# Attention and a two-layer network in one kernel: the third score tile turned by VectorE through DRAM, the fourth by direct moves from two queues, the first as one plain float32 product

## The chip, the core and the metric

The kernel runs on one core of a Trainium2 chip. The metric is the device time of one execution in microseconds (us); lower is better. The engines are TensorE (PE in the profile; PEld is its weight loads), VectorE (DVE), ScalarE (ACT), GpSimd (POOL) and SyncE (SP), which here only issues DMA transfers. They run side by side, each working through its own list of instructions in a fixed order, and wait for one another on semaphores.

## The reference

Attention with a decay that is computed from `f`, for 8 x 8 heads, 576 positions and 64 values per head, then a network of two layers with a leaky activation (cut):

```python
def _attn_ref(q, k, v, f):          # q, k, v: (8, 8, 576, 64); f: (8, 8, 576)
    scores = scale * np.matmul(q, k.transpose(0, 1, 3, 2))
    cum = np.cumsum(np.log(np.clip(f, 0.0001, 1.0)), axis=-1)
    decay = cum[:, :, :, None] - cum[:, :, None, :]
    scores = np.where(causal, -1000000000.0, scores + decay)
    attn = np.exp(scores - np.max(scores, axis=-1, keepdims=True))
    attn = attn / (np.sum(attn, axis=-1, keepdims=True) + 1e-09)
    return np.matmul(attn, v)
def _moe_ref(x, w_in, w_out, alpha):   # x: (4608, 512), w_in: (512, 2048), w_out: (2048, 512)
    h = x @ w_in
    g = np.maximum(h, 0.0) + alpha * np.minimum(h, 0.0)
    return g @ w_out
```

## The kernel before, in words

**Stages.** Attention goes in 32 stages, one for each pair of heads of a batch (`attention(n)`, `n` = 0 to 31). A stage has the rows of its scores in tiles: tiles 0 to 3 are 128 queries of one head against the 128, 256, 384 or 512 keys that the mask lets through, and the tail is the last 64 queries of both heads together against all 576 keys. For each tile TensorE forms the scores, VectorE adds the decay and mask (`Z`) and finds the row's extreme (L674, the tail L571), ScalarE takes the exponential and the row sums (L536).

**Terms.** From stage `NN` = 4 on, the float32 q and k are split into a high and a low part (ScalarE copies the high one, L496; GpSimd subtracts for the low one, L497), and a score is the sum of three products `Qh Kh`, `Qh Kl`, `Ql Kh`. Stages 0 to 3 use one plain float32 product.

**Turning.** The product with `v` needs the exponentials with keys on the partitions, so each 128 x 128 block has to be transposed. In a stage that is not turned all blocks are transposed by TensorE (L549, L718) into a PSUM bank and copied out by ScalarE (L545) or VectorE. In a *turned* stage (`NX[0] <= n < NX[1]`, stages 9 to 31) the fourth tile of both heads and the tail are written to a DRAM tile `ex` in one transfer (L694), read back in four with blocks of keys rearranged over the partitions (L696), and then turned by VectorE in blocks of 32 x 32 (L703, L706) into `eT3`. The order of keys differs from the plain one, so these stages load a `v` with rows in that order (`vt`). Tiles 0, 1, 2 and the tail's last 64 keys are still transposed by TensorE.

**Values.** The products with `v` of a stage are appended to the scores of tile 2 of the stage after it (`behind`, in `stretch`), and ScalarE copies them out (L755). They are scaled by the reciprocal row sums on VectorE (L767) and split into high and low part (L769 on ScalarE, L771 on GpSimd) into one of seven `xx` slots.

**The network.** `ffn1(b)` multiplies the four `xx` slots of a batch by the split `w_in`: 16 blocks of twelve products with 512 columns. Its batches are the filler: the planner gives them low priority, so that TensorE takes them when attention has nothing ready. A ninth pass takes the last 64 rows of all batches. Each block's result goes to DRAM (`hd`, L853). After attention its memory is given up (`change`), `w_out` is loaded and converted in eight chunks (`load_w_out`, L987 to L1014, mostly VectorE and ScalarE), and `ffn2` does the second layer in 18 units of four groups.

**The order of the work.** `Plan` holds every operation with its engine, estimated nanoseconds, key, dependencies and buffers. `Plan.run` simulates the engines: it takes the operation that can start first, at equal start that of lowest key, and issues it. Thus the order on each engine is fixed when the program is built. Transfers also occupy a common channel in this plan, at 220 and later 280 GB/s; the plan counts only transfers of SP in it. `Ring` and `Store` are pools of buffers; a buffer is taken when an operation starts and is free when its last user ends. Once the last stage that is not turned is through, `swap` hands buffers that turned stages no longer need to other rings.

Of the kernel before, what the change touches and what calls it, by code (L numbers as in the profile page):

```python
# [23 lines left out]
QW = 640  # L24
# [6 lines left out]
NX = (9, B * NP)  # L31
NZ = 1+9
NQ = 4
HURRY = 25
# [52 lines left out]
class Plan:  # L87
# [30 lines left out]
    def run(self):  # L118
# [7 lines left out]
        while left:  # L126
# [63 lines left out]
def attention_moe(  # L190
    ctx: ExitStack,
    tc: tile.TileContext,
    qk: bass.AP,
    vv: bass.AP,
    vt: bass.AP,
    f: bass.AP,
# [19 lines left out]
    ex = [dram.tile([3, 128, 512], F32, name=f"ex{i}") for i in range(2)]  # L216
# [34 lines left out]
    rvr = ring(sp, 2, [128, 8, 2, D], F32, "vr")  # L251
# [12 lines left out]
    re = ring(sp, 3, [128, S], F32, "e")  # L264
# [170 lines left out]
    def load_n(n, held):  # L435
# [8 lines left out]
        l_qk = [op("SP", 450, lambda c0=c0, c1=c1: sy.dma_start(bqk.t[:, c0:c1], qk[b, p][:, c0:c1]), kq, dq, [bqk], kb=(c1 - c0) / 2)  # L444
                for c0, c1 in (((0, QW), (QW, QW + S)) if n < NQ else ((0, QW + S),))]
# [43 lines left out]
        if n < NN:  # L489
            held += [bqk]  # L490
            return l_qk, rz, rt, bZ, [(q_, k_)]
# [3 lines left out]
        for hi, lo, raw, w, ld in ((Qh, Ql, q_, QW, l_qk[0]), (Kh, Kl, k_, S, l_qk[-1])):  # L495
            o1 = op("ACT", c_acs(w), lambda hi=hi, raw=raw: ac.activation(hi(), raw(), AF.Copy), kc, [ld], [bqk, bQ])  # L496
# [3 lines left out]
        return out, rz, rt, bZ, [(Qh, Kh), (Qh, Kl), (Ql, Kh)]  # L500
# [3 lines left out]
    def attention(n):  # L504
# [8 lines left out]
        rdy, rz, rt, bZ, terms = load_n(n, held)  # L513
        bv, turned = Buf(rvr), NX[0] <= n < NX[1]
        if turned:
            l_v = op("SP", 400, lambda: sy.dma_start(bv.t, vt[b, p]), kl + 12, [o_scan], [bv], kb=512)
        else:
            l_v = op("SP", 400, lambda: sy.dma_start(bv.t[:, 0:5], vv[b, p]), kl + 1, [o_scan], [bv], kb=320)
# [3 lines left out]
        t2_of = (lambda h: bT2[h].t[:, h]) if turned else (lambda h: bT2[h].t[:, 0:3, 0:128])  # L522
        b3, bT3 = Buf(re3), Buf(rT3)
        if turned:
            bm = Buf(rm3)
# [26 lines left out]
        e2, e3 = [[], []], []  # L552
# [3 lines left out]
        def tail(st):  # L556

            bt = b3 if turned else Buf(re)
# [18 lines left out]
            if turned:  # L577
                return bt, nt
# [8 lines left out]
        e4 = None  # L587
# [49 lines left out]
        def stretch(tiles, st):  # L637

            part = [(i, bool(i >= 2 and len(tiles) > 1), 128 if i == 1 else 0) for i in tiles]
            bS = [[Buf(rS) for _ in range(2)] for _ in range(1 + part[-1][1])]  # L640

            def prods():
                for i, g, c0 in part:
                    w = 128 * i + 128
                    for c, (q, k) in enumerate(terms):
                        for h in range(2):
                            r = slice(64 * h, 64 * h + 64)
                            mm(bS[g][h].t[:, c0 : c0 + w], q()[r, 128 * i : 128 * i + 128], k()[r, 0:w], c == 0, c == len(terms) - 1)
# [4 lines left out]
            s = op("PE", ns, lambda: (prods(), vp()), st, rdy + vd, [x for y in bS for x in y] + held + vb)  # L653
            s_0.append(s)
            if after:
                value_ops.append(s)
            done(s)
            if n == NE - 1 and tiles[-1] == 3:
                op("-", 0, lambda: setattr(rS, "least", 4), 0, [s])
            return {i: (bS[g], c0) for i, g, c0 in part}, s  # L660

        def tile(h, i, st, bS, s, c0):
# [3 lines left out]
            b1 = b3 if i == 3 else Buf(res if i < 2 else re)  # L666
            at = (lambda t: t[:, 512 * h : 512 * h + 512]) if i == 3 else (lambda t: t)
# [21 lines left out]
            if i == 3 and turned:  # L689
                if h == 0:  # L690
                    return
                key = k0 + 7.8
                d = ex[n % 2]
                o_ = op("SP", 400, lambda: sy.dma_start(d.rearrange("g q k -> q g k"), b3.t[:, 0:1536].rearrange("p (g k) -> p g k", g=3)),  # L694
                        key, [be[0][3][1], nm, nt], [b3], kb=768)
                got = [op("SP", 400, lambda k=k: sy.dma_start(  # L696
                    bm.t[32 * k : 32 * k + 32], d[:, :, 128 * k : 128 * k + 128].rearrange("g (a c) s -> c (g a) s", c=32)),
                    key + 0.1, [o_], [bm], kb=256) for k in range(4)]
                for g in range(3):
# [9 lines left out]
                    e3.append(op("DVE", c_tr(512) + 100 * (g == 2), turn, k0 + 13.5, got, [bm, bT3]))  # L709
# [18 lines left out]
        def prods_of(r, out):  # L728

            def pv():  # L730
                both = []
                o = out()
                for h in range(2):
# [3 lines left out]
                    else:  # L737
                        t3 = bT3.t[:, :, 192 * h : 192 * h + 192]
                        head = [(j, 0, 128, e2_[:, j]) for j in range(3)]
                        if turned:  # L740
                            both.append(head + [(j + 4, 128, 320, t3[:, j]) for j in range(3)] + [(3, 256, 320, bT4.t[:, 64 * h : 64 * h + 64])]
                                        + [(7, 128, 320, t3[:, 3])])
# [15 lines left out]
        v_deps = lambda: e1 + e2[0] + e2[1] + e3 + [e4, o_zero, l_v]  # L758
# [40 lines left out]
        if n < NE - 1 or n == B * NP - 1:  # L799
            vb, vp, vd, done = values()  # L800
            done(op("PE", ns_v + 250, vp, k0 + 9.6 - hurry, vd, vb))
        else:
            behind.append(values)
# [77 lines left out]
    o_ct = [op("POOL", c_po(S) + 60, lambda h=h: sides(h), kc_ + 3, [o_cq]) for h in range(2)]  # L881
    for n in range(NX[0], B * NP):
        attention(n)
        if n == NX[0]:
            def swap():
                for st, t in [(rT2b.store, t2s[:, i, 0:768].rearrange("p (h j q) -> p h j q", h=2, q=128)) for i in range(2)] + [
                        (re3.store, t2s[:, 2:4].rearrange("p a n -> p (a n)"))]:
                    st.free.append((plan.t, len(st.items)))
                    st.items.append(t)

            op("-", 0, swap, 0, [value_ops[-1]])
# [78 lines left out]
    def load_w_out(c):  # L970
        key = 1e5 + c
# [175 lines left out]
_ARGS = ["qk", "vv", "vt", "f", "w_in", "w_out", "alpha"]  # L1147
# [37 lines left out]
```

## Time and profile before

| | |
|---|---|
| median of 3 runs | 1058.59 us (1058.38 to 1058.63) |
| the profiled execution's own time | 1056.91 us |
| its span | 1054.7 us |
| granted TensorE clock | 0.995 |
| transfers of `ex` | 23 writes of 768 KB, 92 reads of 192 KB |
| transfers of q and k | 8 in the first four stages, 28 of 608 KB after them |
| HBM read, written | 125.41 MB, 66.61 MB |

A group row of the profile has the line, engine, operation, `out<-in` by the program's names, the shapes and a count; then the busy time and the mean ns of one; then the engine's idle time just ahead and what ended it. A timeline row has the start and the length in us. In the chain that ended last each row is the start and length of a piece of work that the next one had to follow. `eT__114` in the rows is the second buffer of `e3`, which `swap` added.

### The profile page before, as it was taken

Reading aid. Unit: us, or ns where it says so; the run is one execution under the profiler, and the core shown is the slowest. Engines: PE = TensorE matmul, PEld = TensorE weight load, DVE = VectorE, ACT = ScalarE, POOL = GpSimd, SP = SyncE. Lnnn points to the kernel's source line nnn. Section 1 sums busy time; section 2 is a strip of 40 time slices with the busy share of each in tenths; the row PEclk is TensorE's granted clock in tenths of the full one; section 3 lists DMA queues with packets and bytes.
Section 4 is the critical chain, followed back from the end, with each engine's and each line's share of the span. In section 5 each row is a group of like instructions: output and inputs, shape, how many; then the busy total and the mean of one; then the engine's idle time right before and its main releaser. Section 6 shows DMA issues by size and latency. Waiting matters only on the chain.

```text
span 1054.7 us, 21382 instructions
## 1 busy us (share of the span) xinstructions
PE 1041.1 (99%) x7680; PEld 901.6 (85%) x7680; DVE 797.8 (76%) x1772; ACT 661.7 (63%) x1546; POOL 283.6 (27%) x411
## 2 busy tenths in 40 slices
PE   8889999999999999999999999999999999999998
PEld 4578888778778787877788888899999999999998
DVE  6887876667667666757753697789889888989994
ACT  6878885677676767676754566656464554645551
POOL 6586765355344444453510000000000000000000
PEclk9989999999999999999999999999999999999999
DMA  5867757877687678787764667364434434344411
GB/s 182 255 207 219 237 185 215 251 222 222 211 254 237 201 222 249 243 209 217 216 171 149 211 223 237 141 210 134 136 121 143 137 121 142 121 139 126 135 61 41
DMA packets 148820, 193.87 MB, mean 184 GB/s; under 512 B 16723, under 2 KB 98122, under 8 KB 148714
## 3 DMA queue, kind: packets, MB, share of 16 engines
q1 hardware_dynamic: 148425, 192.31, 60.4%
q8 instruction: 60, 0.98, 0.4%
q14 instruction: 47, 0.38, 0.1%
q10 hardware_dynamic: 288, 0.20, 0.1%
HBM read 125.41 MB, written 66.61 MB: 182 GB/s over the span
## 4 chain that ended last, share of the span: by engine, by line
PE 96%; DVE 2%; POOL 1%; ACT 0%; issue 0%; DVEq 0%
PE bank L342 90%; PE bank L549 5%; PE bank L402 1%; PE bank L718 0%; DVE wr L332 0%; DVE wr L329 0%; DVE xs L767 0%; PE bank L618 0%; DVE wr L333 0%; DVE e L674 0%; POOL Z L469 0%; ACT es L536 0%; DVE eT L544 0%; DVE eT__114 L544 0%; POOL wi L338 0%
## 5 line engine op out<-in xcount | busy, mean ns | idle before, releaser
L342 PE MATMUL bank<-xx,wi 128*128 128x512 f32 x1728 | 427.0, 397 | 0.0
L342 PEld LDWEIGHTS bank<-xx,wi 128*128 128x128 f32 x1728 | 314.7, 188 | 65.8 <-issue 4.9
L851 DVE SCALAR_TENSOR_TENSOR hs<-bank,sa,hs 128x512 f32<-128x512 f32 x96 | 71.7, 747 | 117.2 <-ACT hs L849 116.7
L342 PE MATMUL bank<-wot,xx 128*128 128x256 f32 x1008 | 123.9, 283 | 0.0
L342 PE MATMUL bank<-wi,xx 128*128 128x256 f32 x1008 | 123.9, 283 | 0.0
L342 PEld LDWEIGHTS bank<-wot,xx 128*128 128x128 f32 x1008 | 122.3, 192 | 0.0
L342 PEld LDWEIGHTS bank<-wi,xx 128*128 128x128 f32 x1008 | 122.3, 192 | 0.0
L849 ACT ACTIVATE hs<-bank,ab 128x512 f32<-128x512 f32 x96 | 65.9, 686 | 70.1 <-PE bank L342 69.5
L469 POOL TENSOR_TENSOR Z<-Z,tri 128x384 f32<-128x384 f32 x64 | 61.4, 966 | 106.6 <-DVE Z L453 90.3
L536 ACT ACTIVATE e<-e,st 128x384 f32<-128x384 f32 (+2 forms) x127 | 84.8, 672 | 2.9 <-issue 1.1
L771 POOL TENSOR_TENSOR xx<-xs,xx 128x256 fp32r<-128x256 f32 x64 | 49.2, 779 | 131.6 <-ACT xx L769 131.6
L1073 ACT ACTIVATE xx<-gx 128x1024 fp32r<-128x1024 f32 x48 | 50.8, 1058 | 30.6 <-PE bank L342 12.7
L342 PE MATMUL bank<-eT,vr 128*64 128x192 f32 (+3 forms) x896 | 69.3, 303 | 0.0
L1076 DVE TENSOR_TENSOR xx<-gx,xx 128x1024 fp32r<-128x1024 f32 x48 | 58.5, 1219 | 8.2 <-ACT xx L1073 8.2
L342 PE MATMUL bank<-wi,gh 128*128 128x256 f32 x504 | 62.4, 283 | 0.0
L342 PE MATMUL bank<-wot,gh 128*128 128x256 f32 x504 | 62.4, 283 | 0.0
L342 PEld LDWEIGHTS bank<-eT,vr 128*64 128x64 f32 x896 | 55.1, 137 | 8.1
L342 PEld LDWEIGHTS bank<-wot,gh 128*128 128x128 f32 x504 | 61.4, 192 | 0.1
L342 PEld LDWEIGHTS bank<-wi,gh 128*128 128x128 f32 x504 | 61.3, 192 | 0.0
L755 ACT ACTIVATE xs<-bank 128x320 f32<-128x320 f32 (+1 forms) x64 | 25.5, 409 | 56.9 <-PE bank L342 29.3
L497 POOL TENSOR_TENSOR Ql<-rqk,Qh 128x640 fp32r<-128x640 f32 x28 | 45.4, 1620 | 57.4 <-ACT Qh L496 44.5
L342 PE MATMUL bank<-Kh,Qh 64*128 64x128 f32 (+1 forms) x280 | 60.4, 365 | 0.0
(156 smaller groups left out, 1889.1 us busy)
## 6 DMA issues: line engine op xcount, KB each, us to landing
hd<-hs SPq DMA_DIRECT2D x144, 256.0 KB, 3.6
wx<-hd SPq DMA_DIRECT2D x47, 512.0 KB, 3.7
wr<-ex SPq DMA_DIRECT2D x92, 192.0 KB, 4.8
rqk<-in_qk_dram SPq DMA_DIRECT2D x28, 608.0 KB, 4.4
hr<-hd SPq DMA_DIRECT2D x25, 512.0 KB, 4.0
vr<-in_vt_dram SPq DMA_DIRECT2D x23, 512.0 KB, 5.3
ex<-e SPq DMA_DIRECT2D x12, 768.0 KB, 5.2
ex<-eT__114 SPq DMA_DIRECT2D x11, 768.0 KB, 4.5
```

The source lines that it names most:

```text
L342: pe.matmul(o, lhsT, rhs, start=start, stop=stop)
L402: op("PE", 800, lambda: [pe.matmul(bw.t, wbf[:, 0:128], wbf, start=True, stop=True) for _ in range(3)], -200, [o_wbf], [bw])
L469: m1 = op("POOL", c_po(128 * 3), lambda z4=z4: po.tensor_tensor(z4()[:, 6:9], z4()[:, 0:3], tb(3), ALU.add), kc + 0.1, got + [o_mask], [bZ])
L497: o2 = op("POOL", c_po(w), lambda hi=hi, lo=lo, raw=raw: po.tensor_tensor(lo(), raw(), hi().bitcast(F32), ALU.subtract), kc, [o1], [bqk, bQ])
L536: ex = op("ACT", c_exp(w), lambda: ac.activation(at(bt.t)[:, :w], at(bt.t)[:, :w], AF.Exp, bias=lo()[:, col : col + 1], scale=-1.0, accum_ ...
L549: pe.transpose(t[:, c : c + 128], src[:, 128 * j : 128 * j + 128], ident)
L755: xs_ops[r].append(op("ACT", c_act(w_), lambda: ac.activation(bxs[r].t, bP.t[:, 0:w_], AF.Copy), st, [pvo], [bP, bxs[r]]))
L771: xl = op("POOL", c_po(256), lambda r=r, t0=t0: po.tensor_tensor(bx.t[:, 1, t0 : t0 + 256], bxs[r].t[:, 0:256], bx.t[:, 0, t0 : t0 + 256]. ...
L849: cp = op("ACT", c_act(512), lambda bh=bh, bs=bs, fc=fc: ac.activation(bs.t, bh.t, AF.Relu, scale=ab[:, fc : fc + 1]), -1000, [last, o_sg] ...
L851: cp = op("DVE", c_dve(512), lambda bh=bh, bs=bs, fc=fc: ve.scalar_tensor_tensor(bs.t, bh.t, sa[:, fc : fc + 1], bs.t, ALU.mult, ALU.add), ...
L1073: his.append(op("ACT", c_acs(128 * GW * (j1 - j0)), lambda j0=j0, j1=j1, src=src, o_=o_: ac.activation(o_(0, j0, j1), src(), AF.Copy), key ...
L1076: rdy.append(op("DVE", c_dve(128 * GW * (j1 - j0)), lambda j0=j0, j1=j1, src=src, o_=o_: ve.tensor_tensor(o_(1, j0, j1), src(), o_(0, j0, ...
```

## The change

- The turned stages begin with stage 10 (`NX`), as does the way in which `Z` is filled there (`NZ`).
- In turned stages tile 2 of both heads is written to DRAM (`ex2`), read back in four transfers and turned by VectorE in one instruction of 768 columns; TensorE's transposes and ScalarE's copies of it are gone. The tail's last 64 keys are transposed alone.
- The fourth tile and the tail no longer pass through DRAM: 16 transfers, each of 32 partitions, move them straight to the place where the reads put them; they are issued in turn by SP and GpSimd.
- In turned stages tile 0's scores are one plain float32 product of the raw q and k, which are held until then.
- In turned stages tiles 2 and 3 come first, and 0 and 1 after them with the values of the stage before.
- From stage 4 on q and k come in two transfers (`qk1`, `qk2`); in turned stages `v` comes in two (`vt`, `vu`), in a single buffer that has ten blocks, three of them for the key order of tile 2.
- `swap` comes ahead of the first turned stage and waits for the values of the stage before; it now hands out the memory of `e` and `v` too.
- In `Plan` transfers of every queue count in the channel. Chunks 4 to 7 of `w_out` get keys among the groups of the first `ffn2` unit (`WC`).

The diff, cut to its core:

```diff
-NX = (9, B * NP)
-NZ = 1+9
+NX = (10, B * NP)
+NZ = 1+10
+WC = 4
...
-            if o.eng == "SP":
+            if o.kb:
...
-    ex = [dram.tile([3, 128, 512], F32, name=f"ex{i}") for i in range(2)]
+    ex2 = [dram.tile([2, 128, 384], F32, name=f"exs{i}") for i in range(2)]
...
+        else:
+            l_qk = [op("SP", 500, lambda: sy.dma_start(bqk.t[:, 0:1024].rearrange("p (c n) -> p c n", c=2), qk1[b, p].rearrange("c p n -> p c n")), kq, dq, [bqk], kb=400),
+                    op("SP", 500, lambda: sy.dma_start(bqk.t[:, 1024:], qk2[b, p]), kq, dq, [bqk], kb=96)]
...
         if turned:
-            l_v = op("SP", 400, lambda: sy.dma_start(bv.t, vt[b, p]), kl + 12, [o_scan], [bv], kb=512)
+            l_v = [op("SP", 500, lambda: sy.dma_start(bv.t[:, 0:8].rearrange("p (c j) h d -> p c (j h d)", c=2), vt[b, p].rearrange("c p n -> p c n")), kl + 12, [o_scan], [bv], kb=400),
+                   op("SP", 500, lambda: sy.dma_start(bv.t[:, 8:10], vu[b, p]), kl + 12, [o_scan], [bv], kb=128)]
...
+                tt = op("PE", 109, lambda: pe.transpose(bTt.t[0:64, 0:128], tail_of(bt.t)[:, 512:S], ident), st + 1.3, [nt, o_id], [bTt, bt])
+                e4 = op("ACT", c_act(128), lambda: ac.activation(bT4.t[0:64], bTt.t[0:64, 0:128], AF.Copy), st + 1.31, [tt], [bTt, bT4])
...
-                    for c, (q, k) in enumerate(terms):
+                    these = [raw[:2]] if raw and i == 0 else terms
+                    for c, (q, k) in enumerate(these):
...
-            after = behind.pop() if tiles == (2,) and behind else None
+            after = behind.pop() if tiles == ((0, 1) if turned else (2,)) and behind else None
...
-                key = k0 + 7.8
-                d = ex[n % 2]
-                o_ = op("SP", 400, lambda: sy.dma_start(d.rearrange("g q k -> q g k"), b3.t[:, 0:1536].rearrange("p (g k) -> p g k", g=3)),
-                        key, [be[0][3][1], nm, nt], [b3], kb=768)
-                got = [op("SP", 400, lambda k=k: sy.dma_start(
-                    bm.t[32 * k : 32 * k + 32], d[:, :, 128 * k : 128 * k + 128].rearrange("g (a c) s -> c (g a) s", c=32)),
-                    key + 0.1, [o_], [bm], kb=256) for k in range(4)]
+                key = k0 + 4.8
+                src = lambda a, k: b3.t[32 * a : 32 * a + 32, 0:1536].rearrange("p (g s) -> p g s", g=3)[:, :, 128 * k : 128 * k + 128]
+                dst = lambda a, k: bm.t[32 * k : 32 * k + 32].rearrange("p (g a) s -> p g a s", a=4)[:, :, a]
+                got = []
+                for j in range(16):
+                    a, k = j // 4, j % 4
+                    q_, e_ = ((sy, "SP"), (po, "POOL"))[j % 2]
+                    got.append(op(e_, 600, lambda a=a, k=k, q_=q_: q_.dma_start(dst(a, k), src(a, k)), key + j / 100, [be[0][3][1], nm, nt], [b3, bm], kb=60))
...
+            if i == 2 and turned:
+                if h == 0:
+                    return
+                d2 = ex2[n % 2]
+                key = k0 + 2.2
+                o_ = op("SP", 500, lambda: sy.dma_start(d2.rearrange("h q k -> q h k"), be2.t.rearrange("p (h k) -> p h k", h=2)),
+                        key, [be[0][2][1], nm], [be2], kb=336)
+                got = [op("SP", 500, lambda k=k: sy.dma_start(
+                    bm2.t[32 * k : 32 * k + 32], d2[:, :, 96 * k : 96 * k + 96].rearrange("h (a c) s -> c (h a) s", c=32)),
+                    key + 0.1, [o_], [bm2], kb=148) for k in range(4)]
+                e2[0].append(op("DVE", c_tr(768), lambda: ve.transpose(
+                    bT2[0].t.rearrange("p s (a c) -> p a s c", c=32), bm2.t.rearrange("p a (s r) -> p a s r", r=32)), k0 + 8.4, got, [bm2, bT2[0]]))
                 return
...
-        k_ = (0, 2, 6, 8) if n < NE else (0, 2, 8, 6)
+        k_ = (0, 2, 6, 8) if n < NE else (7, 7.5, 0, 2) if turned else (0, 2, 8, 6)
-        for tiles in ((0, 1), (2,), (3,)) if n < NE else ((0, 1, 3), (2,)):
+        for tiles in ((0, 1), (2,), (3,)) if n < NE else ((2, 3), (0, 1)) if turned else ((0, 1, 3), (2,)):
...
-        key = 1e5 + c
+        key = 1e5 + c if c < WC else 2e6 + c // 2 - 0.5
```

More of the change, by code (lines that the diff above doesn't have):

```diff
@@ L193, in attention_moe @@
     qk: bass.AP,
+    qk1: bass.AP,
+    qk2: bass.AP,
     vv: bass.AP,
     vt: bass.AP,
+    vu: bass.AP,
     f: bass.AP,
@@ L250, in attention_moe @@
     rZ = Ring(Store([(sp.tile([128, 2, ZW], F32, name=f"Z{i}"), sp.tile([128, S], F32, name=f"Zt{i}")) for i in range(2)]))
-    rvr = ring(sp, 2, [128, 8, 2, D], F32, "vr")
+    vrt = sp.tile([128, 10, 2, D], F32, name="vr")
+    rvr = Ring(Store([vrt[:, 5 * i : 5 * i + 5] for i in range(2)]))
+    rvt = Ring(Store([]))
     rT1 = ring(sp, 3, [128, 384], F32, "eT1_")
@@ L263, in attention_moe @@
     rT4 = ring(sp, 2, [128, 128], F32, "eT4_")
-    re = ring(sp, 3, [128, S], F32, "e")
+    es_ = sp.tile([128, 3 * S], F32, name="e")
+    re = Ring(Store([es_[:, S * i : S * i + S] for i in range(3)]))
+    re2, rm2 = Ring(Store([])), Ring(Store([]))
     re3 = ring(sp, 1, [128, 1024 + S], F32, "e3_")
@@ L499, in load_n @@
         held.append(bQ)
-        return out, rz, rt, bZ, [(Qh, Kh), (Qh, Kl), (Ql, Kh)]
+        return out + l_qk, rz, rt, bZ, [(Qh, Kh), (Qh, Kl), (Ql, Kh)], (q_, k_, bqk) if n >= NX[0] else None
     waiting, behind, later_x, quick_ops, value_ops = [], [], [], [], []
@@ L521, in attention @@
         bT2 = [Buf(rT2b)] * 2 if turned else [Buf(rT2) for _ in range(2)]
-        t2_of = (lambda h: bT2[h].t[:, h]) if turned else (lambda h: bT2[h].t[:, 0:3, 0:128])
+        t2_of = (lambda h: bT2[h].t[:, :, 128 * h : 128 * h + 128]) if turned else (lambda h: bT2[h].t[:, 0:3, 0:128])
         b3, bT3 = Buf(re3), Buf(rT3)
         if turned:
-            bm = Buf(rm3)
+            bm, be2, bm2 = Buf(rm3), Buf(re2), Buf(rm2)
         bT4, bst = Buf(rT4), Buf(rst)
@@ L584, in tail @@
             return bt, nt
-        e4 = None
         xs_ops = [[], []]
@@ L637, in stretch @@
         def stretch(tiles, st):
-            part = [(i, bool(i >= 2 and len(tiles) > 1), 128 if i == 1 else 0) for i in tiles]
+            part = [(i, int(i >= 2 and i != tiles[0]), 128 if i == 1 else 0) for i in tiles]
             bS = [[Buf(rS) for _ in range(2)] for _ in range(1 + part[-1][1])]
@@ L665, in tile @@
             w = 128 * i + 128
-            b1 = b3 if i == 3 else Buf(res if i < 2 else re)
-            at = (lambda t: t[:, 512 * h : 512 * h + 512]) if i == 3 else (lambda t: t)
+            b1 = b3 if i == 3 else be2 if i == 2 and turned else Buf(res if i < 2 else re)
+            at = (lambda t: t[:, w * h : w * h + w]) if i == 3 or i == 2 and turned else (lambda t: t)
             col = 5 * h + i
@@ L738, in pv @@
                         t3 = bT3.t[:, :, 192 * h : 192 * h + 192]
-                        head = [(j, 0, 128, e2_[:, j]) for j in range(3)]
+                        head = [(j + 7 * turned, 0, 128, e2_[:, j]) for j in range(3)]
                         if turned:
-                            both.append(head + [(j + 4, 128, 320, t3[:, j]) for j in range(3)] + [(3, 256, 320, bT4.t[:, 64 * h : 64 * h + 64])]
-                                        + [(7, 128, 320, t3[:, 3])])
+                            both.append(head + [(j + 3, 128, 320, t3[:, j]) for j in range(3)] + [(2, 256, 320, bT4.t[:, 64 * h : 64 * h + 64])]
+                                        + [(6, 128, 320, t3[:, 3])])
                         else:
@@ L881, in attention_moe, with swap @@
     o_ct = [op("POOL", c_po(S) + 60, lambda h=h: sides(h), kc_ + 3, [o_cq]) for h in range(2)]
+    def swap():
+        for st, t in [(rT2b.store, t2s[:, i, 0:768].rearrange("p (s q) -> p s q", q=256)) for i in range(2)] + [
+                (re3.store, t2s[:, 2:4].rearrange("p a n -> p (a n)")), (re2.store, es_[:, 0:768]), (rvt.store, vrt),
+                (rm2.store, es_[:, 768:1536].rearrange("p (k s) -> p k s", s=96))]:
+            st.free.append((plan.t, len(st.items)))
+            st.items.append(t)
+    op("-", 0, swap, 0, [value_ops[-1]])
     for n in range(NX[0], B * NP):
         attention(n)
[L884 to L891, printed above, removed]
     done_a = [o for o in plan.ops if o not in set(x_late)]
@@ L1144, in attention_moe @@
     plan.run()
-_ARGS = ["qk", "vv", "vt", "f", "w_in", "w_out", "alpha"]
+_ARGS = ["qk", "qk1", "qk2", "vv", "vt", "vu", "f", "w_in", "w_out", "alpha"]
 def kernel(**inputs):
```

46 lines of the change are left out of this document (29 added, 17 removed).

## The prediction

> **What bounds the kernel now.** I read the page first: busy time by engine, then the chain that ended last.
>
> ```profile
> span 1054.7 us, 21382 instructions
> ...
> PE 1041.1 (99%) x7680; PEld 901.6 (85%) x7680; DVE 797.8 (76%) x1772; ACT 661.7 (63%) x1546; POOL 283.6 (27%) x411
> ...
> PE 96%; DVE 2%; POOL 1%; ACT 0%; issue 0%; DVEq 0%
> ```
>
> TensorE is busy for 99% of the span and carries 96% of the chain. A share can hide stages, so the windows view comes next; its columns are the length, busy time of TensorE, its weight loads, VectorE, ScalarE, GpSimd, then granted clock, DMA share and GB/s.
>
> ```profile
> 75.00:165.00 90.00, 90.00 (x761) 73.36 (x759) 66.52 (x160) 79.52 (x214) 60.03 (x73) 1.00 0.71 219
> 300.00:475.00 175.00, 175.00 (x1254) 139.27 (x1252) 115.89 (x306) 119.40 (x326) 77.67 (x108) 1.00 0.78 228
> 602.00:689.00 87.00, 87.00 (x390) 72.19 (x389) 69.83 (x121) 55.14 (x83) 0.62 (x1) 1.00 0.58 197
> ```
>
> From 75 us on TensorE never stops at the full clock, because products of the first feed-forward layer (xx,wi) fill every hole that attention leaves. In the turned stages VectorE is busy 66% of the time, ScalarE 68%, GpSimd 44%, the DMA engines 78%. So work taken off TensorE shortens the kernel one for one, as long as filler is there. The timeline shows one turned stage, from one tile-2 product to the next:
>
> ```profile
> 306.43 0.44 PE L342 MATMUL bank<-Kh,Qh 64*128 64x384 f32 x2
> ...
> 310.01 1.66 PE L342 MATMUL bank<-xx,wi 128*128 128x512 f32 x6
> 311.61 0.33 PE L342 MATMUL bank<-Kh,Qh 64*128 64x128 f32 x2
> 311.77 0.27 PE L342 MATMUL bank<-Kl,Qh 64*128 64x128 f32 x2
> 311.88 0.28 PE L342 MATMUL bank<-Kh,Ql 64*128 64x128 f32 x2
> ...
> 313.59 1.64 PE L342 MATMUL bank<-xx,wi 128*128 128x512 f32 x6
> 315.07 0.49 PE L549 MATMUL bank<-ident,e 128*128 128x128 f32 x3
> 315.32 1.64 PE L342 MATMUL bank<-xx,wi 128*128 128x512 f32 x6
> ...
> 317.70 2.90 PE L342 MATMUL bank<-xx,wi 128*128 128x512 f32 x12
> 320.43 0.81 PE L549 MATMUL bank<-ident,es 128*128 128x128 f32 x6
> 321.00 1.62 PE L342 MATMUL bank<-xx,wi 128*128 128x512 f32 x6
> 322.55 0.44 PE L342 MATMUL bank<-Kh,Qh 64*128 64x384 f32 x2
> ```
>
> Twelve filler products take 2.73 us from start to start (317.70 to 320.43), 0.2275 each. Of this stage's 16.12 us, 36 fillers are 8.19, so attention costs TensorE 7.93 us. One stage brings four filler blocks of twelve, 10.92 us. TensorE could use 18.85 us a stage.
>
> **How fast attention goes.** Its last step per stage is a VectorE transpose, whose first and last timeline rows are:
>
> ```profile
> 179.31 0.76 DVE L706 STREAM_TRANSPOSE eT<-wr 128x256 f32<-128x256 f32 x2
> 570.16 0.73 DVE L706 STREAM_TRANSPOSE eT<-wr 128x256 f32<-128x256 f32 x2
> ```
>
> Twenty-two intervals in 390.85 us: 17.77 us a stage, under 18.85, so attention runs ahead of the filler by about 1.1 us a stage. This lead is what the change eats into.
>
> **The change: TensorE.** 22 turned stages remain (23 now); each loses six tile-2 transposes. The chain view prices them by runs of different length:
>
> ```profile
> 93.12 1.02 PE bank L549 x8
> 161.44 0.48 PE bank L549 x3
> ```
>
> Five more transposes are 0.54 us, 0.108 each. 22 x 6 x 0.108 = 14.3 us. The other end: a run of three between fillers (313.59 to 315.32, less six fillers of 0.2275) costs 0.365 us, 0.12 each, or 16.1 us. I take 14.3. The seventh transpose, of the tail, stays, as do the values' shapes. Stage 9 stops being turned and gets back eight transposes for tile 3 and four for the tail: 12 x 0.108 = +1.3 us.
>
> Tile 0 goes from three split products to one plain one. The plain one is in the timeline of the first stage:
>
> ```profile
> 8.87 0.49 PE L342 MATMUL bank<-rqk 64*128 64x128 f32 x4
> ```
>
> Four instructions end after 0.49 us; the split six run from 311.61 to 311.88 + 0.28, 0.55 us. 22 x 0.06 = 1.3 us. Two switches between kinds of product could cost that back; at most the start spacing saves 0.38 - 0.22 = 0.16, 3.5 us (0.22 is the 0.49 without the last one's 0.27 of tail). I take 1.3. The sum is -14.3 + 1.3 - 1.3 = -14.3 us.
>
> **What lies beside it.** ScalarE loses two evacuations and VectorE gains one turn of 768 columns per stage:
>
> ```profile
> L545 ACT ACTIVATE eT__114<-bank 128x384 f32<-128x384 f32 x64 | 31.2, 487 | 6.9 <-PE bank L718 3.8 <-PE bank L549 2.7
> L453 DVE STREAM_TRANSPOSE Z<-wr 128x1024 f32<-128x1024 f32 x22 | 27.4, 1244 | 0.7
> ```
>
> That is -0.97 us and, at three quarters of 1244, +0.95 us. VectorE goes from 66% to some 72%: nothing, unless attention's pace becomes its own.
>
> Queues: the fourth tile loses its write and four reads on SP and gets 16 moves, eight on SP and eight on GpSimd; the third tile brings one write and four reads; q/k and v come in two loads each. SP: +8 +2, five replaced by five.
>
> ```profile
> L696 SPq DMA_DIRECT2D wr<-ex x92: 303/461/1087, 167.8 to 561.8; - x92
> L694 SPq DMA_DIRECT2D ex<-e x12: 370/371/387, 158.1 to 555.4; - x12
> ```
>
> Both rows give least, median and greatest duration in ns. The list of DMA issues has size and time to landing:
>
> ```profile
> wr<-ex SPq DMA_DIRECT2D x92, 192.0 KB, 4.8
> ...
> ex<-e SPq DMA_DIRECT2D x12, 768.0 KB, 5.2
> ```
>
> Ten more at 0.46 is +4.6 us per stage on SP, which does no other work; but it issues in order, so behind each waiting move stand the filler's stores and the next loads. The path: today write and read land 5.2 + 4.8 us apart in sequence; a direct move is one landing, so tile 3 gains up to 5 us of slack, while tile 2 now needs both. The new order (2, 3 first; 0, 1 last with the stage before's values) gives both exchanges nearly a stage. The bytes: tile 3 768 KB moved once instead of twice, tile 2 384 KB twice, v 128 KB more: 128 KB more of some 3 MB, against 22% idle. I cost transfers at nothing.
>
> GpSimd: no row shows a DMA issued there. By SP's rows one costs 0.30 to 1.09 us; I take 0.6, above SP's median, since it has elementwise work too. GpSimd works 77.67 us per 175, 7.9 us per 17.77; with 8 x 0.6 it is 12.7, inside the stage. It would be full at 1.2 us per move. Behind the moves, which wait for the last exponential, stand the next stage's mask sums and low halves, on which its scores wait; two buffers of each let them be done a stage ahead.
>
> The Trainium skill, "SBUF — State Buffer", section "SBUF: two separate sides", says that a DMA issued from GpSimd needs descriptors written by its cores, which wait while VectorE holds the shared port: 620 ns alone, about 3100 beside a copy. By the first figure the moves cost an estimated 5.0 us a stage and the sum stands; by the second, 24.8 us, and GpSimd paces attention. This trace shows the port's other side: VectorE's two-input products of L767 spread as below (min, median, max in ns), so the two engines do get in each other's way; which figure holds for a move no row says, and rival 2 carries it.
>
> ```profile
> L767 DVE TENSOR_TENSOR xs<-xs,ri x64: 380/482/1826, 39.1 to 586.2; 128x256 f32<-128x256 f32 x32, 128x320 f32<-128x320 f32 x32
> ```
>
> **The hand-over.** After attention VectorE converts w_out while TensorE does the last filler:
>
> ```profile
> 591.68 0.42 DVE L990 TENSOR_SCALAR wx<-wr 128x512 uint32<-128x512 uint32 x1
> ...
> 684.28 2.17 DVE L1014 TENSOR_TENSOR wi<-wx,wi 128x768 fp32r<-128x768 f32 x2 [4.50 <-ACT wi L1013]
> ```
> ```profile
> 688.01 2.19 PE L342 MATMUL bank<-wot,gh 128*128 128x256 f32 x17
> ```
>
> It ends at 686.45; the second layer starts at 688.01 and needs the last pair only after three groups of 42 products, at about 0.12 us each 15 us later. With 14.3 us less on TensorE that need moves from 703 to 689: 2.4 us of cover left if attention ends when it does now. Moving chunks 4 to 7 behind the first group's inputs orders the work by need. I cost it at nothing, with this thin cover.
>
> **Sum.** The profiled execution took 1056.91 us; 1056.9 - 14.3 = 1042.6. The median of the runs is 1058.59, 1.7 above it, so 1044.3 us. The 0.25 us by which the three runs differ is far below 0.2%, 2.1 us, which I take as the least that counts.
>
> **Rivals.**
>
> 1. *A thin cover breaks.* Attention's pace slips by some tenths (VectorE's extra turn, SP's ten issues, a single v buffer, later stages that wait for the swap after stage 9). For: the 2.4 us above. Against: attention has 0.7 us less TensorE time to wait for per stage. A slip of 0.3 to 0.6 us over 22 stages is 7 to 13 us, less 2.4: 1049 to 1055.
>
> 2. *Slower: GpSimd paces attention.* Where: its queue in the turned stages. At a price c per move the stage is 7.9 + 8c; against today's 17.77, 22 stages end 22 x (8c - 9.9) later, and beyond 2.4 us this passes to the end. It cancels the 14.3 at c = 1.33; at 1.4 it gives 1044 + 27 = 1071. If each move also waited out VectorE's hold on the port by as much as the slowest L767 exceeds the fastest, 1.45 us, c is 2.05 and the time 1186; this is the skill's rule as a mechanism here, with 2 of this rival's 12 in 100. For: the moves stand in order in front of work that scores need. Against: SP's worst was 1.09, and only two such products of VectorE come per stage.
>
> 3. *Slower or equal: late exchanges.* TensorE's order is fixed, so a value product that waits 0.7 us in each stage undoes everything (15.4 us): 1060; 1 us gives 1066. For: reads of third-tile rows of 384 bytes, smaller than today's 512, and 16 more semaphores. Against: today's waits for the exchange are VectorE's, not TensorE's.
>
> 4. *More is saved*: transposes at 0.12 and tile 0 at 0.16 give -18.3: 1040.
>
> That the transposes stay cannot be: the code has no other branch for a turned tile 2.
>
> **How the numbers follow.** Forecast (1041 to 1047) 0.45; more saved 0.06; thin cover 0.21; no change to be measured 0.07; GpSimd 0.12; late exchanges 0.09. Faster is 0.72, within 2.1 us of 1058.6 0.07, slower 0.21. The range from 1040 to 1066 takes in rivals 1 and 4, no change and the milder half of 3 and leaves out GpSimd and little else; the likeliest case's own is 1041 to 1047.
>
> **What would show it.** L549 falls by 120 runs of one transpose and TensorE still has no idle time after 75 us; the moves on GpSimd near 0.6 us; last turn near 570 us or before; first product of the second layer near 674 us. Wrong if TensorE waits in the turned stages for a bank filled late by GpSimd's low halves, for a turn behind an exchange, or after 660 us for a converted w_out.

## The result, and the profile after

The changed kernel takes 1061.66 us (median of 14 runs, 1059.1 to 1065.87) against 1058.30 us before (14 runs): a ratio of 1.0038, 95% interval 1.0026 to 1.005. It is slower by 0.4%, where 1044.3 us was forecast. The profiled execution took 1060.45 us.

The page of the changed kernel, the lines that answer to the first ones shown of before:

```profile
span 1058.7 us, 21817 instructions
...
PE 1032.9 (98%) x7532; PEld 891.5 (84%) x7532; DVE 808.3 (76%) x1788; ACT 647.1 (61%) x1506; POOL 378.5 (36%) x587
...
PE 84%; DVE 4%; DMA 4%; ACT 3%; SPq 2%; issue 1%; POOL 1%; DVEq 0%; ACTq 0%
```

TensorE works 8.2 us less and the kernel still ends later; its share of the chain that ended last falls from 96% to 84%, and VectorE, DMA, ScalarE and SyncE's queue come in. That is the first thing to see: the chain now leaves TensorE. The windows view has the same columns as in the prediction; its first row here is the kernel before, the others are the changed one:

```profile
75.00:690.00 615.00, 615.00 (x4166) 496.11 (x4165) 420.07 (x1024) 420.06 (x1063) 233.33 (x319) 1.00 0.72 215
75.00:690.00 615.00, 603.21 (x4008) 482.64 (x4007) 431.76 (x1047) 405.36 (x1023) 329.46 (x496) 1.00 0.72 218
375.00:382.00 7.00, 2.84 (x14) 2.03 (x13) 2.62 (x6) 3.50 (x9) 2.17 (x3) 1.00 0.74 181
382.00:389.00 7.00, 7.00 (x58) 5.38 (x59) 3.57 (x7) 1.89 (x5) 6.45 (x10) 0.76 0.88 243
```

From 75 to 690 us TensorE now idles for 615 - 603.21 = 11.8 us; before it had none there. The longest hole lies in 375 to 382 us. The view of waits, for TensorE in 75 to 690 us (columns: total us, times, longest), names who was late:

```profile
PE bank L594 <- ACT eT__113 L550: 5.3, 3, 4.2
PE bank L594 <- ACT e L550: 1.6, 2, 1.3
PE bank L563 <- ACT es L550: 1.2, 2, 1.1
PE bank L563 <- ACT e L550: 1.1, 1, 1.1
...
PE bank L350 <- DVE eT L725: 0.6, 1, 0.6
```

L594 is the lone transpose of the tail, which the change put into TensorE's order by itself; L563 are the other transposes; L550 is the exponential. Exponentials account for 9.2 us of the 11.8, a turned value behind an exchange (L725) for 0.6. The chain of work, followed back through the longest hole (columns: start, length, what; `eT__113` is the second buffer of `e3` here):

```profile
368.39 0.73 DVE Zt L467
...
372.24 7.30 DMA rqk<-in_qk_dram
...
379.56 0.41 ACT Qh L508
...
380.61 0.57 ACT Kh L508
381.18 0.77 ACT eT__113 L550 x2
...
381.99 0.30 PE bank L594
```

Read from below: the transpose waits for an exponential, which stands on ScalarE behind two copies of the next stage's q and k. The load of these took 7.3 us from issue to landing (3.7 to 4.9 before), and ScalarE stood idle for the last 3.5 us of it. The plain product that had kept the buffer ended at 361.7 us; SyncE then issued 14 other transfers before this load. Only this one stop, 4.16 of the 11.8 us, has the load itself in its chain. Most of the others, followed back in the same way, come to a move or a run of issues on SyncE: the one that ends at 287.01 us follows a move that took 4.51 us (`wr<-eT__113`, from 278.90). The view of the instructions on one tile (duration in ns: least, median, greatest; then first and last start) shows how late the loads were. First the kernel before:

```profile
L444 SPq DMA_DIRECT2D rqk<-in_qk_dram x36: 332/352/1377, 1.4 to 492.2; - x36
L496 ACT ACTIVATE Qh<-rqk x28: 720/726/762, 43.5 to 522.8; 128x640 fp32r<-128x640 f32 x28
```

and the changed one:

```profile
L456 SPq DMA_DIRECT2D rqk<-in_qk_dram x28: 378/384/532, 38.8 to 538.4; - x28
L508 ACT ACTIVATE Qh<-rqk x28: 719/738/780, 43.4 to 543.2; 128x640 fp32r<-128x640 f32 x28
```

The last load was issued 30.6 us ahead of its copy before, and 4.8 us after. Pairing every load with its copy in the last 20 stages gives medians of 30.6 and 5.3 us. The prefetch is gone, and ScalarE waits for loads: the same view of the changed kernel counts ScalarE's idle time ahead of these copies (us, times), where before has no such entry.

```profile
  DMA rqk<-in_qk_dram: 20.3, 13
```

### The profile page after: what moved, and what is told of

It is laid out like the page before. It is cut to its first block, busy times and chain, and to the rows that moved or that the text cites. A ratio compares the mean times of both kernels' runs of the same rounds, so it can differ in the third digit from the quotient of the medians.

```text
span 1058.7 us, 21817 instructions
## 1 busy us (share of the span) xinstructions
PE 1032.9 (98%) x7532; PEld 891.5 (84%) x7532; DVE 808.3 (76%) x1788; ACT 647.1 (61%) x1506; POOL 378.5 (36%) x587
## 4 chain that ended last, share of the span: by engine, by line
PE 84%; DVE 4%; DMA 4%; ACT 3%; SPq 2%; issue 1%; POOL 1%; DVEq 0%; ACTq 0%
PE bank L350 79%; PE bank L563 3%; SPq L717 1%; DMA wr<-eT__113 1%; DMA wr<-e 1%; PE bank L410 1%; DMA rqk<-in_qk_dram 1%; DVE xs L799 1%; DMA wr<-in_w_in_dram 1%; DVE wr L340 0%; ACT es L550 0%; DVE wr L337 0%; ACT e L550 0%; PE bank L594 0%; POOL Z L481 0%
## 5 line engine op out<-in xcount | busy, mean ns | idle before, releaser
L550 ACT ACTIVATE e<-e,st 128x384 f32<-128x384 f32 (+2 forms) x127 | 84.9, 670 | 17.4 <-DVE st L692 11.2
L550 ACT ACTIVATE es<-es,st 128x128 f32<-128x128 f32 (+1 forms) x128 | 56.7, 446 | 11.0 <-DVE st L692 10.8
L722 DVE STREAM_TRANSPOSE eT<-wr 128x512 f32<-128x512 f32 x44 | 29.4, 695 | 41.3 <-DMA wr<-e 12.1
```

The source lines that it names most:

```text
L550: ex = op("ACT", c_exp(w), lambda: ac.activation(at(bt.t)[:, :w], at(bt.t)[:, :w], AF.Exp, bias=lo()[:, col : col + 1], scale=-1.0, accum_ ...
L722: ve.transpose(o, bm.t[:, 4 * g : 4 * g + 4].rearrange("p a (s r) -> p a s r", r=32))
```

## The experiments

Four ideas of the cause, as the expectations name them. Q: SyncE's in-order queue is nearly full. L: the landings of the transfers themselves are late. O: the planned order reckons landings too early. G: GpSimd paces attention. After the second set came H: the plain product holds the raw q/k buffer. Each kernel was timed over five rounds beside the kernel before; ratios below are to it, with 95% intervals.

### All moves on GpSimd, and all on SyncE

```
-                    q_, e_ = ((sy, "SP"), (po, "POOL"))[j % 2]
+                    q_, e_ = (po, "POOL")        # the other kernel: (sy, "SP")
```

> All 16 moves of the fourth tile are issued by GpSimd, none by SyncE; the rest is the changed kernel (1061.7 us). Theory Q (SyncE's in-order queue is nearly full in the turned stages, so loads and exchange reads are issued late and TensorE's fixed order stalls): 8 issues of some 0.6 us leave SyncE in each of 22 stages, about 4.8 us of its 18.3 us; most of TensorE's extra idle of some 13 us goes: 1047 to 1055 us. Theory G (GpSimd paces attention): 8 more moves of 0.55 us put GpSimd at 7.9 + 16 x 0.55 = 16.7 us of 18.3 us per stage, in order: 1063 to 1075 us. Theory L (the trips through DRAM and the landings themselves take too long, whoever issues them): no change, 1060 to 1063 us.

Measured: 1053.91 us, ratio 0.9966 (0.9949 to 0.9983). G falls: with twice the moves on GpSimd the kernel gets faster. Its moves in this run:

```profile
L717 POOL DMA_DIRECT2D wr<-e x176: 545/545/712, 183.5 to 565.0; - x176
L717 POOL DMA_DIRECT2D wr<-eT__113 x176: 545/545/592, 204.2 to 580.5; - x176
```

L falls too in its plain form, as the same transfers with the same bytes cost 7.8 us less from another queue. The loads are still late here (a median of 7.5 us ahead of their copies).

> All 16 moves are issued by SyncE, none by GpSimd; else the changed kernel (1061.7 us; with all 16 on GpSimd 1053.9). Theory Q (SyncE's queue): 8 more issues of some 0.6 us in each of 22 stages fill SyncE from 72% to over 95% of a stage of 18.3 us; the idle of TensorE grows by 1 to 2 us per stage: 1075 to 1105 us. If the gain with all moves on GpSimd came from GpSimd's landings being shorter, or from one queue instead of two in the turn's waits, and not from SyncE's load: 1053 to 1063 us.

Measured: 1130.98 us, ratio 1.0678 (1.0659 to 1.0697), worse than expected. Q holds in its direction: SyncE's load matters, and sharply at this level, where its issues fill 303.0 of the 360 us from 200 to 560 us (84%).

### The four q/k and v loads issued by GpSimd

```
-  op("SP", 500, lambda: sy.dma_start(bqk.t[:, 0:1024]...     (and the three other q/k and v loads)
+  op("POOL", 600, lambda: po.dma_start(bqk.t[:, 0:1024]...
```

> The two q/k loads and the two value loads of each turned stage are issued by GpSimd instead of SyncE; moves and exchange stay as in the changed kernel (1061.7 us). Theory Q (SyncE's queue): 4 issues of some 0.5 us leave SyncE per stage and the q/k loads no longer stand behind moves and exchanges: 1049 to 1057 us, and the q/k copies on ScalarE no longer wait for their load. Theory L (landing latency): the exchange reads are as late as before, 1060 to 1063 us. Theory G (GpSimd paces): 4 x 0.55 us more on GpSimd per stage, 1063 to 1068 us.

Measured: 1067.53 us (1058.87 to 1074.06), ratio 1.008 (1.0044 to 1.0117). This was a miss for Q, and the hint that something else was in play: the loads had left SyncE's queue and were hardly earlier for it. The time lies in the range of G, which the run with all moves on GpSimd speaks against. The rows are of the slowest of the eight runs, 1074.06 us:

```profile
L456 POOL DMA_DIRECT2D rqk<-in_qk_dram x28: 704/713/872, 40.4 to 540.3; - x28
...
L508 ACT ACTIVATE Qh<-rqk x28: 719/738/750, 47.5 to 547.3; 128x640 fp32r<-128x640 f32 x28
```

Still 7.0 us from the last issue to its copy (median 6.7).

### The third tile on TensorE again; the fourth through DRAM again

```
-            if i == 2 and turned:                              (third tile: exchange and turn)
+            if False:
-                for j in range(16): ... dma_start(dst(a, k), src(a, k))
+                o_ = ... dma_start(d, b3)                      (fourth tile: one write,
+                got = [... for k in range(4)]                   four reads, as before)
```

> The third tile is turned by TensorE again (6 transposes in each of 22 stages, no trip through DRAM); the fourth tile's direct moves, the plain first tile, the split loads and the stage order of the changed kernel stay. TensorE has some 14 us more work than in the changed kernel (1061.7 us). If the third tile's trip (5 more SyncE issues, its landing wait on VectorE) makes the stalls: the idle goes with it and the work comes back, 1056 to 1061 us. If the stalls come from the direct moves or from the order: idle stays and the work is added, 1070 to 1077 us.

Measured: 1060.28 us, ratio 1.0024 (1.0016 to 1.0033). TensorE gets its 14 us of transposes back and the kernel is not slower: the third tile's trip, as it stood in this order, was paid for with about as much waiting as it saved. TensorE idles only 2.5 us here, although ScalarE waits 20.0 us for q/k loads. So late loads alone need not stop TensorE.

> The fourth tile goes through DRAM again (one write and four reads by SyncE in each of 22 stages instead of 8 moves by SyncE and 8 by GpSimd); the third tile's trip through DRAM, the plain first tile and the split loads stay as in the changed kernel (1061.7 us). If the direct moves on SyncE are the cost: most of the 13 us of idle goes, 1046 to 1052 us. Theory Q (count of SyncE's issues, 3 fewer per stage): part of it, 1052 to 1059 us. If the third tile's trip alone is the cost: 1060 to 1063 us. If a trip through DRAM is what is late (theory L), two trips are worse than one: 1063 to 1075 us.

Measured: 1077.89 us, ratio 1.019 (1.0173 to 1.0207). So the direct moves are no loss against a second trip through DRAM, which costs more although SyncE then has fewer issues than with the moves (406 in 200 to 560 us against 491). Why is taken up again below.

### SyncE loaded in the kernel before

```
+                for j in range(10):
+                    op("SP", 500, lambda j=j: sy.dma_start(dm[n, j], ident[0:32]), key + j / 100, [...])
```

> The kernel before, whole, and in each of its 23 turned stages 10 more transfers of 32 x 512 B from an idle tile to unused DRAM, issued by SyncE where the exchange is issued; nothing waits for them. Theory Q (issues alone fill SyncE's in-order queue, from 37% to some 65%): loads and exchange reads behind them are late, TensorE idles: 1061 to 1072 us. If SyncE's load alone does no harm, and only transfers on which the turn waits are late: 1057 to 1060 us.

Measured: 1069.24 us, ratio 1.0109 (1.0096 to 1.0122). Transfers that nothing waits for do harm, with the q/k loads early (29.3 us in the median). They stood right in front of the exchange reads, and VectorE's wait for these grew; first the row of the kernel before, then of this one (waits of VectorE in 75 to 690 us):

```profile
DVE eT L703 <- DMA wr<-ex: 6.9, 7, 1.9
```
```profile
DVE eT L706 <- DMA wr<-ex: 73.4, 20, 5.0
```

### The same operations, planned for later landings

```
-                end = self.chan + 1.0
+                end = self.chan + (1.0 if s < FAR or o.kb > 700 else 3.0)
```

> The changed kernel with the order replanned: every transfer after 90 us is reckoned to land 3.0 us after its bytes instead of 1.0, so turns, copies and products that wait for a landing are put later in the engines' orders; no instruction is added or removed. Theory O (the order reckons landings too early, and VectorE and ScalarE stand in line behind them): waits on landings shrink, 1050 to 1058 us. Theory Q alone (the queue is full, so what is late stays late): 1059 to 1064 us.

Measured: 1071.05 us, ratio 1.0134 (1.0114 to 1.0154). O falls: reckoning landings later made it worse, by more than Q alone allows. A new order by itself can move this kernel by several us.

### The first tile split again

```
-        ..., (q_, k_, bqk) if n >= NX[0] else None
+        ..., None
```

> The first tile's scores are the three products of split factors again; else the changed kernel (1061.7 us). By the profile's rows the plain product saves TensorE some 0.06 us per stage, 1.3 us in all, and holds the raw q/k buffer longer, so that the load after next is issued later. If that hold delays the q/k loads: faster than the changed kernel, 1056 to 1060 us. If it is harmless: 1062 to 1064 us.

Measured: 1051.53 us, ratio 0.9935 (0.9917 to 0.9952): 10 us faster than the changed kernel, faster than the kernel before, and below the 1056 to 1060 expected, with SyncE as loaded as ever. The part that the forecast priced at a gain of 1.3 us was a loss of ten. In this run the loads are early again, 26.1 us ahead of the last copy:

```profile
L456 SPq DMA_DIRECT2D rqk<-in_qk_dram x28: 378/390/540, 38.8 to 496.1; - x28
...
L508 ACT ACTIVATE Qh<-rqk x28: 719/728/781, 43.3 to 522.2; 128x640 fp32r<-128x640 f32 x28
```

### The hold without the plain product

```
-                    these = [raw[:2]] if raw and i == 0 else terms
+                    these = terms                             (the buffer stays in the product's list)
```

> The first tile's scores are three split products as in the faster variant without the plain product (1051.5 us), but the order still keeps the raw q/k buffer until the stage's (0, 1) product, as the changed kernel does (1061.7 us). Theory H (the plain product's harm is the hold: with two buffers the q/k load is issued only after that product, some 5 us before its use instead of some 20): 1059 to 1064 us, with the q/k loads issued 4 to 8 us ahead of the copies. If the plain product itself does the harm (its instructions, TensorE's clock): 1050 to 1054 us.

Measured: 1066.11 us, ratio 1.0082 (1.0061 to 1.0103). Every engine's order is that of the changed kernel but for the first tile's products. The plain product is gone, the harm is not; the time is even 4.5 us above the changed kernel's, and above the 1059 to 1064 expected:

```profile
L456 SPq DMA_DIRECT2D rqk<-in_qk_dram x28: 378/384/2027, 39.3 to 537.7; - x28
...
L508 ACT ACTIVATE Qh<-rqk x28: 719/739/769, 43.8 to 543.7; 128x640 fp32r<-128x640 f32 x28
```

6.0 us ahead again, and ScalarE waits 25.8 us for loads. This kernel has the same instructions as the split first tile; only the list of buffers differs, and 14.6 us lie between them. So keeping the buffer is what costs. How it costs is shown in part: the longer hold makes the loads late, but it also gives another planned order, and the two have not been separated. (The run planned for later landings shows that an order alone can cost 9.4 us.) Taking the hold away made the kernel faster at every placing of the fourth tile: by 10.1 us with mixed moves, 15.8 through DRAM, 5.6 with all moves on SyncE and 2.1 with all on GpSimd, the last with overlapping intervals.

### Both suspects away

Both edits together, first tile split and all 16 moves on GpSimd; and the same with every fourth move on SyncE.

> The changed kernel with both suspects taken away: first tile from split products (hold gone) and all 16 moves on GpSimd (8 issues off SyncE). Alone these gave 1051.5 and 1053.9 us against 1061.7. Theory H and theory Q as separate causes: 1043 to 1048 us, nearly no idle of TensorE ahead of the second layer. If both act on the same lateness, so that one of them is enough: 1050 to 1053 us. GpSimd, some 90% busy in the attention stages, as the next bound: 1052 to 1060 us.

Measured: 1051.86 us, ratio 0.994 (0.992 to 0.9959). No faster than the split first tile alone: the two gains of 10.1 and 7.8 us do not add up, as expected if both act on the same lateness. Once nothing holds the buffer, taking eight issues off SyncE brings nothing.

> As the variant with split first tile and all moves on GpSimd, but with 4 of the 16 moves on SyncE. If neither queue is full there, it equals that variant within 2 us; if GpSimd's queue limits that one, this is 2 to 5 us faster; if SyncE's issues still cost, 2 to 4 us slower.

Measured: 1054.01 us, ratio 0.9962 (0.9948 to 0.9976), its interval overlapping the other's, though the 2.15 us between them lie at the edge of what was expected of no difference. Neither queue is shown to limit.

### The third tile's turn alone

Fourth tile through DRAM and first tile split.

> The fourth tile goes through DRAM again and the first tile's scores are split products: of the change the third tile's turn by VectorE stays (with the split loads and the stage order). The changed kernel with the fourth tile through DRAM took 1077.9 us. If the hold of the q/k buffer was what hurt there: 1052 to 1060 us. If two trips through DRAM overload the DMA engines (their busy share was 0.82 to 0.91 between 200 and 575 us there, against 0.75 to 0.81 before): 1065 to 1078 us.

Measured: 1062.10 us, ratio 1.0048 (1.0031 to 1.0065), between the two ranges expected. The hold accounts for 15.8 us of the 1077.9; the other 10.6 us, against the split first tile with direct moves, are the fourth tile's second trip. The DMA engines are busier here (share 0.83; the column ahead of GB/s) than in the kernel with direct moves and split first tile, whose row follows:

```profile
75.00:690.00 615.00, 605.10 (x4038) 485.37 (x4037) 425.09 (x1028) 401.70 (x1014) 232.46 (x318) 0.99 0.83 245
```
```profile
75.00:690.00 615.00, 610.18 (x4117) 492.52 (x4115) 445.63 (x1056) 411.46 (x1032) 329.26 (x496) 1.00 0.76 222
```

That the busier engines are what makes it slow, rather than the longer sequence of write and reads, was not separated.

### All moves on SyncE without the hold

> All 16 moves on SyncE, first tile from split products (no hold of the q/k buffer). With the hold all moves on SyncE gave 1131.0 us, 69 more than the changed kernel. If SyncE's load only hurts through the q/k loads that the hold makes urgent: 1051 to 1062 us. If a full queue hurts by itself (exchange reads, stores and moves late): 1085 to 1120 us.

Measured: 1125.39 us, ratio 1.0632 (1.0607 to 1.0656). SyncE's issues fill 308.5 of the 360 us from 200 to 560 us (86%), and that hurts by itself: the q/k loads are early here (32.0 us ahead in the median). VectorE's waits in this run:

```profile
DVE eT__113 L740 <- DMA e<-exs: 63.2, 20, 6.5
DVE eT L722 <- DMA wr<-e: 56.6, 11, 9.2
```

Here it is the turns that are late, and TensorE waits for these (38.3 us for `eT`, ten times). Sixteen moves in one queue are not the harm as such, since GpSimd issues as many in the fast run above.

### The plain product from a copy

```
+            br = Buf(rr0)                                     (a ring of two [128, 256] buffers)
+            out.append(op("POOL", 2 * c_po(128), lambda: [po.tensor_copy(br.t[:, 0:128], q_()[:, 0:128]),
+                                                          po.tensor_copy(br.t[:, 128:256], k_()[:, 0:128])], kc, l_qk, [bqk, br]))
```

> The changed kernel (1061.7 us) with its plain first-tile product and its 8 + 8 moves, but the product reads a copy of the 128 + 128 columns that it needs, made by GpSimd (two copies of 128x128, an estimate of 0.7 us per stage) into a small ring of its own, so the raw q/k buffer is free after the split again. Theory H (the hold alone is the plain product's harm): 1048 to 1053 us, q/k loads issued 10 us or more ahead of the copies again; less than the 1051.5 of the split first tile by up to 1.3 us. If the plain product has another cost in this order: 1057 to 1064 us.

Measured: 1059.16 us (1054.71 to 1064.37), ratio 1.0014 (1.0 to 1.0027). Loads were early again (median 28.7 us), but only 2.5 us of the 10 came back: a miss for H as it was put. So the two copies were put inside the low-half operation and reckoned at nothing, which leaves every engine's order as in the kernel with the split first tile, the copies and the product apart; and the same with the copies unused.

> The plain first-tile product reads a copy, as in the run that gave 1059.2 us, but the two copies are made inside GpSimd's operation for the low half and reckoned at nothing, so that every engine's order is that of the split first tile (1051.5 us) but for the copies and the product itself. If the 1059.2 came from the other order that the copies brought: 1049 to 1053 us. If the copies' 0.7 us on GpSimd per stage or the plain product do harm: 1056 to 1062 us.

> The copies are made as in the kernel with copies inside GpSimd's low-half operation, but the first tile's scores are the three split products, so the copies are not used: the order of the split first tile (1051.5 us) plus the copies alone. If the copies' time on GpSimd is the harm: 1056 to 1062 us. If it is the plain product: 1051 to 1053 us. If neither: 1051 to 1053 us with the plain one 1 us below.

Measured: 1055.35 us, ratio 0.9974 (0.996 to 0.9989), with the plain product; 1056.47 us, ratio 0.9981 (0.9967 to 0.9995), with unused copies. The three readings of the expectations each hold in part: the copies cost 4.9 us (1056.47 against 1051.53), the order that the planner made for them another 3.8 (1059.16 against 1055.35), and the plain product costs nothing: it is 1.1 us below its split twin, though the two intervals overlap. Why two copies of 0.29 us a stage cost 4.9 us was not found out.

## Why the prediction was wrong, step by step

**The step that failed** is the one on the first tile. The forecast priced it by TensorE's time alone, -1.3 us. That term is not refuted: with every order the same, the plain product came out 1.1 us faster from copies, within the noise, and 4.5 us faster with the buffer held. What was left out is the buffer. The product that reads the raw q and k is the last of the stage, `(0, 1)`, and there are two raw buffers; so the load for the stage after next can't be issued until that product has run. The list of changes says so (the raw q and k "are held until then"), and no term of the sum answered to it. Holding the buffer without the plain product gives 1066.11 us, and dropping both gives 1051.53. The lead of the loads fell from 30.6 to 5.3 us, where the prediction left it as it was.

**SyncE's queue** was the second step at fault. "Does no other work" was true and beside the point. The forecast had +4.6 us of issues a stage at 0.46 each. The moves on SyncE take longer:

```profile
L717 SPq DMA_DIRECT2D wr<-e x88: 585/598/1253, 184.1 to 557.8; - x88
...
L717 SPq DMA_DIRECT2D wr<-eT__113 x88: 589/602/680, 197.0 to 574.7; - x88
```

Adding up all of SyncE's issues from 200 to 560 us gives 133.3 us (300 of them) before and 261.0 us (491) after: 37% and 72% of the time, 6.7 us more in a stage; the kernel with the split first tile has 274.5 us, 76%. With the buffer held, what counts is how soon after the product the load gets its turn. It is issued 8.0 us after the product's end (median over the stages) with eight moves on SyncE, and 4.3 us with none; the lead to the copy is 5.3 and 7.5 us. This fits the 7.8 us that taking the moves off SyncE brought with the hold, and the nothing that it brought without it. The prediction named "the next loads" behind each waiting move and gave them no time.

**Transposes.** Their number fell from 524 to 404, the 120 forecast. What this is worth shows where TensorE waits little: with both suspects away (its profiled execution took 1048.31 us, 3.5 below the median) the second layer's first product and the busy time are

```profile
679.36 4.83 PE L350 MATMUL bank<-wot,gh 128*128 128x256 f32 x39
```
```profile
75.00:690.00 615.00, 612.25 (x4144) 494.87 (x4143) 440.25 (x1049) 411.68 (x1030) 423.09 (x672) 1.00 0.75 220
```

It starts 8.65 us earlier than the 688.01 of before, with 2.75 us of idle: 11.4 us of work saved where -14.3 + 1.3 = -13.0 was forecast for it. The term was right to 1.6 us. The mechanism of the gain was right; it was outweighed.

**GpSimd.** 0.6 us a move was forecast; the changed kernel shows

```profile
L717 POOL DMA_DIRECT2D wr<-e x88: 545/545/712, 183.2 to 552.4; - x88
...
L717 POOL DMA_DIRECT2D wr<-eT__113 x88: 545/545/595, 197.3 to 572.0; - x88
```

Rival 2 is out. The Trainium skill ("SBUF — State Buffer", section "SBUF: two separate sides") gives about 620 ns for a DMA issued from GpSimd alone and about 3100 beside a copy of VectorE. These rows are the time on GpSimd's queue: the first figure is near, and no move came near the second, with VectorE busy for two thirds of the time. Which VectorE operation ran beside each move they do not say, so the second figure was not met here rather than refuted.

**The covers.** Rival 1 named a slip of attention's pace by 0.3 to 0.6 us a stage, and attention did slip: the last turn of the fourth tile starts at 579.4 us instead of 570.5.

```profile
L725 DVE STREAM_TRANSPOSE eT<-wr x44: 400/402/432, 195.1 to 579.4; 128x256 f32<-128x256 f32 x44
```

That is (579.4 - 195.1) / 21 = 18.3 us a stage against 17.77. But the pace isn't what decides: with both suspects away the last turn is at 581.5 and the kernel 9.8 us faster. What decides is whether TensorE, whose order is fixed, stops at single products. Rival 3 said so and had the time, 1060 us; its place was wrong. It put the wait at the value products behind an exchange. It was mostly at transposes behind exponentials, the longest of them behind a q/k load. That 1061.66 us lies inside the stated 1040 to 1066 is thus luck more than mechanism. The hand-over to the second layer held at nothing: from its first product, at 691.65 us, to the end are 367.0 us, and 366.7 before.

**What stays open.** The split first tile was forecast, by the same sum, at 1044.3 + 1.3 = 1045.6 us and took 1051.5. It has 4.8 us of idle left, and the work saved fell 1.6 us short of the sum. Whether VectorE's waits for the third tile's reads make this idle was not tested, nor what share of the ten microseconds the planned order has.

## What to carry to other kernels

When an operation is moved to read an earlier form of its data, price the buffer that it now keeps as well as its own time: find which load refills that buffer, and compare the load's new earliest issue with its use. A prefetch that has lost its lead shows as a load in the chain of work and as a shrunken distance between the last issue and the last use in the rows of one tile. A queue that issues in order harms little while its transfers are early (here 76% busy took no longer than 45%) and much once something urgent stands behind the rest: 11.5 us with exchange reads behind ten idle transfers at 67%, 69 and 74 us with all moves on SyncE at 84 and 86%.

## What the runs showed of the hardware

TensorE pays for a long stall twice. After the hole at 377 us in the changed kernel the timeline shows

```profile
381.99 0.30 PE L594 MATMUL bank<-ident,eT__113 128*64 128x128 f32 x1 [4.16 <-ACT eT__113 L550]
382.05 2.61 PE L350 MATMUL bank<-xx,wi 128*128 128x512 f32 x6
```

Six fillers take 2.54 us from start to start (382.05 to 384.59, where the next product begins), 0.42 each instead of 0.2275, and the granted clock in 382 to 389 us is 0.76 (windows row above), 0.50 from 382.4 to 385.8. The Trainium skill ("TensorE: Matmul & The Clock Gate", section "Part 1: The HAM clock gate") has the clock halved after an idle window of about 3.4 us, and the 4.16 us here agree. A shorter hole was followed by the same once: in the kernel with the split first tile TensorE idled 1.5 us in 419 to 422 us and 0.5 us more by 422.8, and the clock fell (the column ahead of the DMA share). Another was not: after 1.35 us of idle ahead of 287.01 us in the changed kernel the clock stayed at 1.00. The rows are of the first:

```profile
419.00:422.00 3.00, 1.53 (x9) 1.16 (x8) 3.00 (x4) 0.00 (x0) 0.85 (x1) 1.00 0.77 160
422.00:426.00 4.00, 3.52 (x12) 2.47 (x11) 4.00 (x13) 3.19 (x9) 4.00 (x5) 0.65 0.73 253
```

The same 48 KB move takes 0.60 us of issue on SyncE and 0.545 on GpSimd, where it stayed between 0.545 and 0.712 us, even with all sixteen there and GpSimd busy for 157.3 of the 175 us from 300 to 475.
